# The 1e-9 of the softmax sums: an add on VectorE in place of an activation on ScalarE

## The chip, the cores and the metric

One core of one Trainium2 chip runs the kernel. The metric is the device time of one execution in microseconds (us), and the figure before is the median of 3 runs. The engines are TensorE (PE in the profile, with its weight loads as PEld), VectorE (DVE), ScalarE (ACT), GpSimd (POOL) and SyncE (SP, which here issues most DMAs).

## The reference

Attention with a local and a summary part, and then a gated feed-forward layer, all in float32:

```
B, H, S, D = 4, 8, 768, 64;  block, window = 32, 16
k_sum = max of k over blocks of 32 keys;  v_sum = mean of v over blocks of 32
scores_l = scale * q k^T, kept where |i - j| < 16, else -1e9
scores_s = scale * q k_sum^T + log(32)
a = exp(concat(scores_l, scores_s) - rowmax)
a = a / (sum(a) + 1e-9)
x = a @ concat(v, v_sum)            -> (4, 768, 512)
h = relu(x @ w_in)                  -> (4, 768, 1024)
conv = 3-tap convolution of h along the sequence, per channel
out = (h * sigmoid(conv)) @ w_out   -> (4, 768, 512)
```

The weights of the feed-forward layer come as 64-bit floats. The kernel decodes them to float32 on the chip.

## The kernel before, in words

The sequence of each of the 4 batches is cut into two halves, which gives 8 chunks of 384 positions (c = 0 to 7). A chunk has 4 pairs of heads, so there are 32 pairs (n = 4c + p, n = 0 to 31). Attention works on blocks of 64 queries; each block sees a window of 96 keys and the 24 summary keys, 120 columns.

For one pair, `qk` (L248) issues 24 small matmuls (L260) of queries against keys into two PSUM tiles `pq`, one per head, and calls `softmax` (L271). For each of the two heads and three column groups, VectorE adds the mask and finds the row's extreme (L278, the value goes to `nm`), and ScalarE takes the exponential with the row sum accumulated into one column of `sm` (L288; the profile shows an ACTIVATE and a read of the accumulator for each). That gives six sums per row, in the 128x6 tile `sm`. ScalarE then adds 1e-9 to all six (L296), VectorE takes the reciprocal (L297), and the exponentials are multiplied by it (L300), on VectorE for the pairs 0 to 3 and on GpSimd for all others. `tr` (L304) transposes them on TensorE (L308) and copies them out (L313, L315); `av` (L320) multiplies by the values (L329), and the result is split into a high and a low part, `xh` on ScalarE (L349) and `xl` on VectorE (L350).

The feed-forward layer uses split numbers: `f1` (L393) multiplies three products of high and low parts (L404) per block of 128 columns; `gate_conv` (L415) applies relu (L422) and the convolution (L425 or L427, then L434 twice); `gate_mul` (L444) does tanh (L451), the product (L452), and the split into `ghi` on ScalarE (L455) and `glo` on GpSimd (L456); `f2` (L462) does the last matmul (L473) and ScalarE writes it out (L482). The weights are decoded and split by `weights` (L124): ScalarE L97, VectorE L100, L101, L104, ScalarE L127, GpSimd L128. `vmean_pair` (L221) and `prep_pair` (L202) make the summary values and keys (VectorE L228 and L210, ScalarE L236, GpSimd L217, L213 and L238).

The order of the work. The program lists the work in units; each unit calls `slot(j)` (L359), in which even j start a pair's `qk` and odd j prepare the next pair, then `slot_t` (transposes of the group two slots before, DEPTH = 2) and `slot_av`, the feed-forward pieces of the unit, and a part of the gate work that is left over. Chunk 0's four pairs come first, before any feed-forward work (L507 to L516). Semaphores are put in by the framework, and the framework also orders the instructions of each engine, by data dependences, the place in the source and estimated durations. Only for chunks 2 to 7 (`ORDERED` is 2) is TensorE's order the order of the source:

```
        if c < ORDERED:
            for u in range(NFC):
                unit(c, u, pieces, False)
        else:
            with tc.manual_schedule(engines={mybir.EngineType.PE}):
                for u in range(NFC):
                    unit(c, u, pieces, True)
```

All other engines, and TensorE in chunks 0 and 1, get their order from the framework. Matmuls on a zero tile (L78, `warm`) stand between the early work. The tiles `sm` and `nm` have 3 buffers each, the exponentials `a` have 4. Each engine works through its queue in order, so an instruction that waits holds up what is behind it on that engine.

Of the kernel before, what the change touches and what calls it, by code (L numbers as in the profile page):

```python
# [10 lines left out]
AF = mybir.ActivationFunctionType  # L11
ALU = mybir.AluOpType
# [38 lines left out]
def attention_ffn(ctx, tc, qT, kT, vT, v4, w_in, cwT, w_out, mask8, ident_in, out):  # L51
    nc = tc.nc
# [195 lines left out]
    def qk(c, p):  # L248


        st = state[(c, p)]
        n = c * NP + p
        pq = [
            ps.tile([P, 512], F32, tag="s", name=f"pq{n}_{h}", bufs=2) for h in range(2)
        ]
        for blk in range(CB):
            i, half = divmod(blk, 2)
            for h in range(2):
                r = slice(h * QB, (h + 1) * QB)
                last = nc.tensor.matmul(  # L260
                    pq[h][half * QB : (half + 1) * QB, i * NK : (i + 1) * NK],
                    st["q"][r, blk * QB : (blk + 1) * QB],
                    st["kw"][r, blk, :],
                    start=True,
                    stop=True,
                )
        if c == 0:
            warm(f"pq{p}", ins(last))
        softmax(n, c % 2, pq)

    def softmax(n, hf, pq):  # L271
        nm = sp.tile([P, 2, 3], F32, tag="nm", name=f"nm{n}", bufs=3)
        sm = sp.tile([P, 2, 3], F32, tag="sm", name=f"sm{n}", bufs=3)
        for h in range(2):
            a = sp.tile([P, 3, NK], F32, tag="a", name=f"a{n}_{h}", bufs=DEPTH + 2)
            state[("a", 2 * n + h)] = a
            for i in range(3):
                nc.vector.tensor_tensor_reduce(  # L278
                    a[:, i, :],
                    pq[h][:, i * NK : (i + 1) * NK],  # L280
                    mask[:, hf, i, :],
                    -0.125,
                    3.0e38,
                    ALU.add,
                    ALU.min,
                    nm[:, h, i : i + 1],
                )
                nc.scalar.activation(  # L288
                    a[:, i, :],
                    a[:, i, :],  # L290
                    AF.Exp,
                    bias=nm[:, h, i : i + 1],
                    scale=-1.0,
                    accum_out=sm[:, h, i : i + 1],
                )
        nc.scalar.activation(sm, sm, AF.Copy, bias=1e-9)  # L296
        nc.vector.reciprocal(sm, sm)  # L297
        for h in range(2):
            a = state[("a", 2 * n + h)]
            (nc.gpsimd if n >= NP else nc.vector).tensor_tensor(  # L300
                a, a, sm[:, h, :].unsqueeze(2).to_broadcast([P, 3, NK]), ALU.mult
            )
# [377 lines left out]
```

## Time and profile before

| | |
|---|---|
| median of 3 runs | 408.15 us (404.59 to 409.48) |
| the profiled execution | 408.03 us, its span 406.2 us |
| granted TensorE clock, mean over the span | 0.986 of full |
| busy: TensorE, its weight loads | 386.4 us, 319.5 us |
| busy: VectorE, ScalarE, GpSimd | 261.3, 254.2, 151.6 us |
| L296: ScalarE, 32 times | 6.6 us busy |
| L297: VectorE, 32 times | 5.9 us busy |
| bytes moved by DMA | 54.47 MB, 134 GB/s on average |

The span runs from the first instruction to the last of one profiled execution; the execution's own time lies 1.8 us above it. All times inside the profile count from the span's start. A busy time sums an engine's instructions; neighbours on one engine can overlap by a tenth of a microsecond, so the start of the next instruction tells more of the engine's pace than the end of the last. The idle time of an engine counts only where the chain of waits runs over it.

### The profile page before, as it was taken

What the parts mean: (1) busy time and instruction counts of PE and PEld (TensorE: products, weight loads), DVE (VectorE), ACT (ScalarE), POOL (GpSimd) and SP (SyncE); (2) the same over time, 40 slices, a digit from 0 to 9 for tenths busy, and PEclk for the clock granted to TensorE, in tenths of its full rate; (3) what the DMA queues carried; (4) which work ended last, traced back from release to release, by engine and by line L of the source; (5) the groups of instructions that cost most, each with busy time, mean ns of one, the idle gap of its engine ahead of it and who ended that gap; (6) DMA issues with size and microseconds to landing.
All of it is one profiled execution on the core that took longest, in us unless ns stands there. A gap on an engine that the chain in (4) does not pass through costs nothing.

```text
span 406.2 us, 8829 instructions
## 1 busy us (share of the span) xinstructions
PE 386.4 (95%) x3164; PEld 319.5 (79%) x3173; DVE 261.3 (64%) x777; ACT 254.2 (63%) x806; POOL 151.6 (37%) x179
## 2 busy tenths in 40 slices
PE   7978869999799999999999999999999999999996
PEld 3546657886678888888888888888788888999884
DVE  4899789998965765668765456466565665556200
ACT  3664799998777677766565777756655654343211
POOL 2327464585953333322432333333332242222200
PEclk9999699999989999999999999999999999999999
DMA  8999863766966774646332344334220000000011
GB/s 290 327 361 211 230 177 115 248 202 192 252 162 205 235 217 123 190 145 192 78 92 78 80 111 112 104 96 117 67 63 28 27 2 26 26 27 26 28 52 52
DMA packets 60715, 54.47 MB, mean 134 GB/s; under 512 B 24640, under 2 KB 51328, under 8 KB 60672
## 3 DMA queue, kind: packets, MB, share of 16 engines
q1 hardware_dynamic: 56928, 47.19, 41.3%
q10 hardware_dynamic: 3744, 6.73, 4.5%
q8 instruction: 25, 0.41, 0.4%
q14 instruction: 18, 0.15, 0.1%
HBM read 45.55 MB, written 6.29 MB: 128 GB/s over the span
## 4 chain that ended last, share of the span: by engine, by line
PE 68%; ACT 11%; DVE 10%; DMA 3%; issue 3%; POOL 3%; SPq 0%; ACTq 0%; DVEq 0%; POOLq 0%
PE f L404 26%; PE f L473 26%; PE pq L260 5%; ACT a L288 5%; PE xp L329 4%; PE pt L308 4%; DVE t L434 3%; PE pw L78 2%; ACT t L451 1%; DMA kw<-kT 1%; DMA k_xh<-kT 1%; ACT f L422 1%; DVE t L452 1%; POOL wout_lo L128 1%; ACT t L425 1%
## 5 line engine op out<-in xcount | busy, mean ns | idle before, releaser
L456 POOL TENSOR_TENSOR glo<-t,ghi 128x383 fp32r<-128x383 f32 (+1 forms) x64 | 66.6, 1041 | 116.3 <-ACT ghi L455 111.8
L434 DVE SCALAR_TENSOR_TENSOR t<-f,cw,t 128x382 f32<-128x382 f32 (+3 forms) x128 | 78.8, 616 | 23.5 <-ACT t L425 20.7
L404 PE MATMUL f<-xh,win_hi 128*128 128x384 f32 (+1 forms) x256 | 93.0, 363 | 0.9 <-ACT win_hi L127 0.9
L404 PE MATMUL f<-xl,win_hi 128*128 128x384 f32 (+1 forms) x256 | 87.7, 343 | 0.0
L404 PE MATMUL f<-xh,win_lo 128*128 128x384 f32 (+1 forms) x256 | 86.9, 340 | 0.0
L473 PE MATMUL f<-wout_lo,ghi 128*128 128x512 f32 x192 | 76.1, 396 | 3.1 <-POOL wout_lo L128 3.1
L288 ACT ACTIVATE a<-a,nm 128x120 f32<-128x120 f32 x192 | 73.3, 384 | 9.1 <-DVE nm L278 8.8
L473 PE MATMUL f<-wout_hi,ghi 128*128 128x512 f32 x192 | 76.3, 398 | 0.2 <-ACT ob L482 0.2
L473 PE MATMUL f<-wout_hi,glo 128*128 128x512 f32 x192 | 75.1, 392 | 0.0
L451 ACT ACTIVATE t<-t 128x383 f32<-128x383 f32 (+1 forms) x64 | 33.6, 525 | 60.4 <-DVE t L434 59.3
L300 POOL TENSOR_TENSOR a<-a,sm 128x360 f32<-128x360 f32 x56 | 45.8, 839 | 64.4 <-DVE sm L297 36.5
L452 DVE SCALAR_TENSOR_TENSOR t<-t,f 128x383 f32<-128x383 f32 (+1 forms) x64 | 35.3, 552 | 28.2 <-ACT t L451 28.2
L404 PEld LDWEIGHTS f<-xh,win_hi 128*128 128x128 f32 x256 | 48.7, 190 | 3.6 <-issue 1.3
L404 PEld LDWEIGHTS f<-xl,win_hi 128*128 128x128 f32 x256 | 49.0, 191 | 0.9 <-issue 0.3
L404 PEld LDWEIGHTS f<-xh,win_lo 128*128 128x128 f32 x256 | 48.8, 191 | 0.2
L278 DVE CUSTOM_DVE_ANT_0 a<-pq,mask 128x120 f32<-128x120 f32 x192 | 42.7, 276 | 1.9 <-PE pq L260 1.9
L473 PEld LDWEIGHTS f<-wout_lo,ghi 128*128 128x128 f32 x192 | 36.3, 189 | 9.7 <-POOL wout_lo L128 4.1
L455 ACT CAST ghi<-t 128x383 fp32r<-128x383 f32 (+1 forms) x64 | 32.6, 509 | 16.6 <-DVE t L452 15.9
L473 PEld LDWEIGHTS f<-wout_hi,glo 128*128 128x128 f32 x192 | 36.2, 188 | 7.7
L473 PEld LDWEIGHTS f<-wout_hi,ghi 128*128 128x128 f32 x192 | 36.1, 188 | 7.3 <-issue 0.6
L308 PE MATMUL pt<-ident,a 128*120 128x128 f32 x192 | 34.0, 285 | 5.4 <-ACT aT L315 3.7
L260 PEld LDWEIGHTS pq<-kw,q 64*64 64x64 f32 x768 | 23.9, 134 | 18.6 <-issue 13.0
(59 smaller groups left out, 505.8 us busy)
## 6 DMA issues: line engine op xcount, KB each, us to landing
va<-v SPq DMA_DIRECT2D x32, 288.0 KB
kw<-kT SPq DMA_DIRECT2D x28, 288.0 KB
q<-qT SPq DMA_DIRECT2D x32, 192.0 KB
out_dram<-ob ACTq DMA_DIRECT2D x24, 256.0 KB
kT<-kT SPq DMA_DIRECT2D x12, 392.0 KB
vt<-vT SPq DMA_DIRECT2D x12, 384.0 KB
wo<-w_out SPq DMA_DIRECT2D x8, 512.0 KB
raw_a<-w_in SPq DMA_DIRECT2D x6, 512.0 KB
```

What stands on the lines that cost most here:

```text
L260: last = nc.tensor.matmul(pq[h][half * QB : (half + 1) * QB, i * NK : (i + 1) * NK], st["q"][r, blk * QB : (blk + 1) * QB], st["kw"][r, bl ...
L278: nc.vector.tensor_tensor_reduce(a[:, i, :], pq[h][:, i * NK : (i + 1) * NK], mask[:, hf, i, :], -0.125, 3.0e38, ALU.add, ALU.min, nm[:, h ...
L288: nc.scalar.activation(a[:, i, :], a[:, i, :], AF.Exp, bias=nm[:, h, i : i + 1], scale=-1.0, accum_out=sm[:, h, i : i + 1],)
L300: (nc.gpsimd if n >= NP else nc.vector).tensor_tensor(a, a, sm[:, h, :].unsqueeze(2).to_broadcast([P, 3, NK]), ALU.mult)
L308: last = nc.tensor.transpose(pt[:NK, i * P : (i + 1) * P], a[:, i, :], ident)
L404: last = nc.tensor.matmul(ph[:, :n], w[:, fc, cc, :], x[:, cc, :n], start=(cc == 0 and m == 0), stop=(cc == NCC - 1 and m == 2),)
L434: nc.vector.scalar_tensor_tensor(t[:, i0:i1], h[:, hf + k - 1 + i0 : hf + k - 1 + i1], cw[:, fc, k : k + 1], t[:, i0:i1], ALU.mult, ALU.add,)
L451: nc.scalar.activation(t, t, AF.Tanh, scale=0.5)
L452: nc.vector.scalar_tensor_tensor(t, t, 1.0, h[:, hf : hf + ng], ALU.add, ALU.mult)
L455: nc.scalar.copy(hi, t)
L456: nc.gpsimd.tensor_tensor(gated["lo"][:, fc, d0 : d0 + ng], t, hi.bitcast(F32), ALU.subtract)
L473: nc.tensor.matmul(po, gx[:, fc, ss], w[:, fc, :], start=(fc == 0 and m == 0), stop=(fc == NFC - 1 and m == 2),)
```

## The change

The addition of 1e-9 to the six sums of a pair is done by VectorE, as a tensor-scalar add in place on the same tile, where ScalarE did it as a copy with a bias. The reciprocal, on VectorE before and after, follows it directly in the source.

```
-        nc.scalar.activation(sm, sm, AF.Copy, bias=1e-9)
+        nc.vector.tensor_scalar(sm, sm, 1e-9, None, ALU.add)
         nc.vector.reciprocal(sm, sm)
         for h in range(2):
             a = state[("a", 2 * n + h)]
```

## Rows read from the trace of the kernel before

**Rows 1.** The page's first part, of the whole span: for each engine its busy time in us, the share of the span and the number of instructions.
```profile
PE 386.4 (95%) x3164; PEld 319.5 (79%) x3173; DVE 261.3 (64%) x777; ACT 254.2 (63%) x806; POOL 151.6 (37%) x179
```

**Rows 2.** The table of busy times by stretch, stretches between 20 and 300 us: the stretch, its length, the busy time of each engine in us (instructions), then TensorE's granted clock as a share of full speed, the mean busy share of the DMA engines, GB/s.
```profile
20.00:30.00 10.00, 8.00 (x94) 4.61 (x95) 9.71 (x30) 6.94 (x25) 1.96 (x2) 1.00 1.04 362
40.00:50.00 10.00, 8.06 (x43) 6.11 (x43) 8.66 (x34) 7.37 (x31) 4.80 (x6) 0.66 0.84 221
44.00:49.00 5.00, 5.00 (x21) 3.65 (x18) 4.16 (x13) 2.74 (x15) 2.27 (x2) 0.50 0.74 218
50.00:60.00 10.00, 6.91 (x108) 5.26 (x108) 7.23 (x31) 9.24 (x32) 6.69 (x8) 1.00 0.77 201
60.00:90.00 30.00, 29.79 (x296) 23.83 (x299) 28.29 (x86) 27.93 (x95) 17.44 (x22) 1.00 0.57 177
150.00:300.00 150.00, 148.18 (x1330) 128.87 (x1328) 92.05 (x298) 99.19 (x323) 53.15 (x69) 1.00 0.40 110
```

**Rows 3.** The list of who waited for whom, whole span: engine, tile and line that waited, what it waited for, us in total, times, the longest.
```profile
DVE sm L297 <- ACT sm L296: 4.8, 6, 2.6
...
PE pt L308 <- POOL a L300: 0.3, 1, 0.3
```

**Rows 4.** The groups of instructions by line, ScalarE's group of L296 and VectorE's of L297: line, engine, operation, out<-in, shapes, count, then busy us and mean ns of one, then idle time just before them and what ended it.
```profile
L296 ACT ACTIVATE sm<-sm 128x6 f32<-128x6 f32 x32 | 6.6, 206 | 0.0
...
L297 DVE RECIPROCAL sm<-sm 128x6 f32<-128x6 f32 x32 | 5.9, 184 | 5.0 <-ACT sm L296 4.8
```

**Rows 5.** The timeline around one pair of the late part, 148 to 157 us (ScalarE, POOL, TensorE): start in us, duration in us, engine, line, operation, out<-in, shapes, count, and in brackets the engine's idle time before it and what ended that.
```profile
148.07 0.19 ACT L288 ACTIVATION_READ_ACCUMULATOR a<-a,nm 128x1 f32 x1
...
148.52 0.21 ACT L296 ACTIVATE sm<-sm 128x6 f32<-128x6 f32 x1
148.63 0.46 ACT L315 COPY aT<-pt 120x384 f32<-120x384 f32 x1
...
149.46 1.54 POOL L300 TENSOR_TENSOR a<-a,sm 128x360 f32<-128x360 f32 x2 [4.15 <-ACT f L422]
...
156.54 0.32 PE L308 MATMUL pt<-ident,a 128*120 128x128 f32 x1
```

**Rows 6.** The timeline around pair 2, ScalarE and VectorE, 19.4 to 20.3 us, columns as in the group before.
```profile
19.39 0.19 ACT L288 ACTIVATION_READ_ACCUMULATOR a<-a,nm 128x1 f32 x1
...
19.84 0.21 ACT L296 ACTIVATE sm<-sm 128x6 f32<-128x6 f32 x1
...
20.08 0.19 DVE L297 RECIPROCAL sm<-sm 128x6 f32<-128x6 f32 x1 [0.95 <-ACT sm L296]
```

**Rows 7.** The chain of waits that ended last, two of its pieces: start in us, its part of the chain in us, engine, tile and line.
```profile
26.28 0.18 DVE sm L297
...
56.29 0.21 ACT sm L296
```

**Rows 8.** VectorE's timeline, small instructions between 15 and 46 us, columns as above.
```profile
15.42 0.56 DVE L313 COPY aT<-pt 120x384 f32<-120x384 f32 x1 [0.76 <-PE pt L308]
...
18.97 0.16 DVE L100 TENSOR_SCALAR wl_cw<-cw_words 128x24 uint32<-128x24 uint32 x1
...
24.84 0.17 DVE L101 SCALAR_TENSOR_TENSOR cw<-cw,wl_cw 128x24 uint32<-128x24 uint32 x1
25.05 0.18 DVE L104 SCALAR_TENSOR_TENSOR cw<-cw_words,cw 128x24 uint32<-128x24 uint32 x1
...
45.20 0.19 DVE L297 RECIPROCAL sm<-sm 128x6 f32<-128x6 f32 x1
45.30 0.24 DVE L278 CUSTOM_DVE_ANT_0 a<-pq,mask 128x120 f32<-128x120 f32 x1
```

**Rows 9.** The timeline of VectorE (first two rows) and of POOL (last three), 11 to 126 us: VectorE's and POOL's instructions that overlap, columns as above.
```profile
35.46 1.28 DVE L344 CAST xl<-xl 128x8 fp32r<-128x8 f32 x1
...
125.01 0.19 DVE L297 RECIPROCAL sm<-sm 128x6 f32<-128x6 f32 x1 [2.63 <-ACT sm L296]
...
11.11 0.82 POOL L238 COPY va<-vm 24x768 f32<-24x768 f32 x1
...
35.41 1.31 POOL L128 TENSOR_TENSOR win_lo<-wu_i,win_hi 128x512 fp32r<-128x512 f32 x1 [1.29 <-ACT win_hi L127]
...
124.94 1.03 POOL L456 TENSOR_TENSOR glo<-t,ghi 128x385 fp32r<-128x385 f32 x1 [2.98 <-ACT ghi L455]
```

**Rows 10.** TensorE's timeline, three instructions that began after an idle stretch, columns as above.
```profile
42.15 0.32 PE L260 MATMUL pq<-kw,q 64*64 64x120 f32 x2 [1.94 <-issue]
...
58.31 0.29 PE L308 MATMUL pt<-ident,a 128*120 128x128 f32 x1 [2.73 <-ACT aT L315]
...
110.41 0.50 PE L473 MATMUL f<-wout_lo,ghi 128*128 128x512 f32 x1 [2.44 <-POOL wout_lo L128]
```

**Rows 11.** The timeline around pair 11, 102 to 105 us (ScalarE, VectorE, POOL), columns as above.
```profile
102.06 0.19 ACT L288 ACTIVATION_READ_ACCUMULATOR a<-a,nm 128x1 f32 x1
...
104.49 0.18 DVE L297 RECIPROCAL sm<-sm 128x6 f32<-128x6 f32 x1
...
104.74 0.79 POOL L300 TENSOR_TENSOR a<-a,sm 128x360 f32<-128x360 f32 x1 [0.73 <-DVE sm L297]
```

**Rows 12.** ScalarE's timeline around 10.5 us, columns as above.
```profile
10.40 0.27 ACT L236 ACTIVATE vm<-pv 24x128 f32<-24x128 f32 x1
10.57 0.19 ACT L296 ACTIVATE sm<-sm 128x6 f32<-128x6 f32 x1
```

More of the change, by code (lines that the diff above doesn't have):

```diff
@@ L295, in softmax @@
                 )
-        nc.scalar.activation(sm, sm, AF.Copy, bias=1e-9)
+        nc.vector.tensor_scalar(sm, sm, 1e-9, None, ALU.add)
         nc.vector.reciprocal(sm, sm)
```

## The prediction

> **What bounds the kernel now.** I read the page first: TensorE (PE) is busy for 95% of the span, VectorE (DVE) and ScalarE (ACT) for 64% and 63% [rows 1]. The reader is to see there that neither engine of the change is the bound as an average. An average hides stages, so the table by stretch comes next [rows 2]. From 150 to 300 us PE has 1.8 us of idle time in 150. In 20 to 30 us it has 2.0 and in 50 to 60 us 3.1, while DVE (9.71 of 10) and then ACT (9.24) are nearly full. From 60 to 90 us all three are nearly full. One more stall, of 2.44 us, ends at 110.41 us [rows 10]. The granted clock is 0.66 of full in 40 to 50 us; within that it is 0.50 from 44 to 49 us, the 1.2 GHz level [rows 2], after PE had stood still for 1.94 us before 42.15 us [rows 10]. The list of waits comes third: PE waited only 0.3 us for the normalised softmax (L300 on POOL) in the whole span [rows 3]. So the change can move the end almost only in the first 125 us, and there only where a softmax pair stands on the chain of waits, which I read last.
>
> **The change part by part.** There are 32 pairs (n = 0 to 31), with one L296 and one L297 each [rows 4].
>
> What it removes. L296 takes 206 ns on ACT [rows 4], but the next instruction starts 0.11 us after it (148.52 and 148.63 us [rows 5]), so ACT gets back about 32 x 0.11 = 3.5 us. One hand-over between engines stays, now from the last sum to the add.
>
> What it adds. The trace has no DVE add of 128x6. The nearest rows are a tensor-scalar of 128x24 with 0.16 us, the reciprocal with 0.18, and, for two small DVE instructions of which the second needs the first, the step from 24.84 to 25.05 us: 0.21 us [rows 8]. I take 0.21 us from add to reciprocal, as these operands are nearest in size. The lower bound is the step from a reciprocal to the next, independent instruction, 0.10 us (45.20 to 45.30 us [rows 8]). The upper bound is 1.28 us, a cast of 8 columns beside a POOL instruction [rows 9]; that is rival 1. On DVE this sums to 32 x 0.21 = 6.7 us, of which few places count.
>
> What it moves. The add needs the last exponential's sum, not L296, and L296 did not follow that sum at once: at 148 us the sum is there at 148.26, L296 starts at 148.52 behind another ACT instruction, and POOL multiplies from 149.46 [rows 5]. So the add can start up to 0.3 us sooner than L296 did. DVE's wait does not grow: before, L297 waited for L296 4.8 us in all, in 6 cases of 32 [rows 3]. Queued behind it on DVE are the convolution (L427, L434) and the next exponents' inputs (L278); ACT and POOL wait for those.
>
> Now the places, against the profiled execution's own 408.03 us (its span of 406.2 and 1.8 around it; the median of the runs is 408.15, so there is no shift to make).
> - Pairs 14 to 31: POOL ends the two multiplications at 151.00 us and PE first transposes one of them two units later, at 156.54 us [rows 5]. These 5.5 us cover both 0.21 us more on DVE and an earlier start. ACT's 0.11 us can matter where PE waits for ACT at all, in the 1.8 us of idle time named above. I take -0.2, bounds -1.8 and 0.
> - Pairs 0 and 1: DVE idles 0.76 us before its copy at 15.42 us [rows 8], which takes both steps of 0.21. Nothing; without that cover +0.4.
> - Pair 2, on the chain: the last sum ends at 19.58, L296 starts at 19.84 and L297 at 20.08, and DVE had been idle for 0.95 us [rows 6]. With the add at 19.62 the reciprocal starts at 19.83: -0.25, bounds -0.4 and 0.
> - Pair 3, on the chain with L297 at 26.28 us [rows 7], where DVE is full [rows 2]: +0.2, bounds 0 and +0.2.
> - Pair 4: L297 at 45.20 us stands between the inputs of the next exponents [rows 8], and POOL follows: +0.1, bounds -0.5 (if the add goes ahead of these) and +0.2.
> - Pair 6: L296 is on the chain at 56.29 us [rows 7], in ACT's run that PE waits 2.73 us for until 58.31 us [rows 10]. One ACT step less: -0.1, bounds -0.36 and 0.
> - Pair 5, where PE runs on at half clock, and 7 to 10, where it is full [rows 2]: nothing.
> - Pair 11: the last sum is there at 102.25, L297 runs only at 104.49 behind a weight decode, POOL idles 0.73 us and multiplies from 104.74; behind that, in POOL's order, come the weights for which PE idles 2.44 us until 110.41 [rows 10, 11]. An add that asks straight after the sum may pass the decode, and POOL's 0.73 us go. If it stays where L297 is, +0.2. I take -0.5.
> - Pairs 12 and 13: PE runs on. Nothing.
> Sum: -0.2 - 0.25 + 0.2 + 0.1 - 0.1 - 0.5 = -0.75 us; the bounds add up to -3.8 and +1.0. Forecast: 408.03 - 0.75 = 407.3 us. What is late next is what is late now: ACT's run to 58 us and the weight splits at 110 us.
>
> **A rule that speaks against it.** First the rows: a cast of 8 columns took 1.28 us from 35.46 us on, beside a POOL instruction of 1.31 us that had begun at 35.41; a reciprocal at 125.01 us, inside a POOL instruction that had begun at 124.94, took 0.19 as ever [rows 9]. The Trainium skill ("SBUF — State Buffer", section "Who interferes with whom") says that VectorE's copy, cast and tensor-scalar, from SBUF to SBUF, can take a pair of ports that GpSimd uses too, and that whichever comes second waits out the other's whole instruction; the reciprocal is not in its list. The trace agrees in both cases. By this the add would pay where the reciprocal behind it does not, which gives rival 1; without it the sum is as above.
>
> **Rivals.**
> 1. Slower: the add waits for a running POOL instruction, as that cast did, and DVE stands behind it. In 10 of the 32 pairs (0, 1, 3, 5, 8 to 13) POOL is running at some time between the last sum and L297 (the first and the last of them in [rows 9]); in the late pairs POOL idles until the multiplication itself (4.15 us before 149.46 [rows 5]), so nothing is paid there. All ten at 1.28 us on the chain would give 408.03 + 12.8 = 420.8; with PE busy in six of them, four count: 408.03 + 4 x 1.28 = 413.2. It decides once 0.75 us of such waits fall on the chain. For it: rows 9. Against it: most of the ten lie where PE has work.
> 2. Slower by another order. The instructions do not run in the order of the source: vmean's copy (L236, at 10.40 us) ran ahead of L296 (10.57), and it is later in the source [rows 12]. The order is worked out from estimated durations, and PE's is fixed by the program only from chunk 2 on. A ready time that moves by 0.1 us may reorder the first 125 us. Price: one stall like that of 2.73 us [rows 10] and one more stretch like that of 10 us at a clock of 0.66, 3.4 us lost [rows 2]: +6.1, about 414 us.
> 3. The same to the good: the stall of 2.44 us [rows 10] and the half-clock stretch go: -5.8, about 402.2 us. For both: two such stalls stand in the present order, so another can have one more or one less. Against both: the last two thirds, where PE's order is fixed, cannot take part.
>
> **How the numbers follow.** Forecast 0.60 (its own range, by the spread of the runs from 404.6 to 409.5, is 405 to 410), rival 1 0.12, rival 2 0.13, rival 3 0.15. The likeliest gives 407.3. A range of 402.5 to 412.5 leaves out some 0.07 below and 0.12 above. A measurement here can tell about 2%, 8.2 us. Under 400.0 needs more than rival 3: 0.04. Over 416.3 needs rival 1 near its upper end or rival 2 with a second stall: 0.06. The rest, 0.90, is within 2%.
>
> **What would show it.** Right: 32 adds of about 0.16 us on DVE, ACT's busy time down by 6.6 us and DVE's up by about 5; L300 of the late pairs 0.3 to 0.6 us sooner after the last sum and no change in PE's pace there; PE's idle time in the first 125 us within 2 us of now. Wrong: adds of 1 us and more (rival 1); another number of half-clock stretches or of stalls over 2 us before 125 us (rivals 2 and 3); a change of length after 150 us by more than the 1.8 us of idle time there, which would break the reading that PE alone sets the pace.

## The result, and the profile after

The changed kernel takes 409.69 us (median of 20 runs, 408.12 to 413.55), the kernel before 408.01 us (20 runs beside it, 404.51 to 410.07). The ratio over all runs is 1.0072 with a 95% interval of 1.0042 to 1.0101, which is about 2.9 us slower, where 0.75 us faster was forecast; the medians lie only 1.7 us apart, the means of the runs 3.0 us. All profiles below are of single executions; the changed kernel's took 410.21 us, its span is 408.4 us. The mean granted clock of this execution and of the one before is the same, 0.986.

A first look at where the time goes. The table gives the end of a unit (its twelfth L404 matmul on TensorE), read off each trace: for the kernel before in us, for the others as the distance from it.

| end of | before | changed | e11 | e12 | e6 | e7 |
|---|---|---|---|---|---|---|
| unit 3 | 61.73 | +1.15 | +1.23 | +0.77 | +3.22 | +0.10 |
| unit 8 | 83.41 | +0.76 | +0.92 | +0.96 | +3.23 | +0.11 |
| unit 10 | 91.81 | +0.21 | +0.93 | +0.38 | +3.23 | +0.11 |
| unit 11 | 96.86 | +3.20 | +0.93 | +3.22 | +3.23 | +0.11 |
| unit 15 | 126.20 | +3.12 | +1.11 | +2.88 | +2.65 | +0.06 |
| unit 39 | 258.41 | +2.61 | +0.90 | +2.71 | +2.64 | -0.41 |
| last instruction | 406.15 | +2.27 | +0.21 | +2.36 | +2.24 | -1.11 |

The second column is the changed kernel; the other four are experiments told below. The loss is there by 126 us, most of it falls on unit 11, between 92 and 100 us, and 0.85 us come back behind it. TensorE's idle time confirms it: from its first instruction to 130 us it sums to 12.9 us in the trace of before and to 16.4 us in that after; behind 130 us it is 2.0 and 1.3 us.

The page's first part of the changed kernel, to be put beside [rows 1]:

```profile
PE 385.8 (94%) x3173; PEld 319.2 (78%) x3173; DVE 269.9 (66%) x809; ACT 251.8 (62%) x774; POOL 150.7 (37%) x179
```

VectorE has 8.6 us more, ScalarE 2.4 us less; TensorE's work is the same. The table by stretch, as [rows 2], of three of its stretches:

```profile
40.00:50.00 10.00, 6.68 (x72) 4.88 (x71) 8.64 (x35) 8.59 (x33) 4.74 (x6) 1.00 0.95 253
...
60.00:90.00 30.00, 29.88 (x274) 24.18 (x273) 27.12 (x84) 25.64 (x86) 16.09 (x20) 0.96 0.54 163
...
150.00:300.00 150.00, 148.70 (x1295) 129.94 (x1294) 94.71 (x308) 100.82 (x321) 52.70 (x69) 1.00 0.43 116
```

From 150 to 300 us TensorE is as full as before. In 40 to 50 us this execution ran at full clock where the one before ran at half for much of the time, and in 60 to 90 us a little slower: where the half-speed stretches fall differs, so the profiles can't be compared stretch by stretch without the clock beside them.

The groups of L296 and L297, as [rows 4], and the waits, as [rows 3]:

```profile
L296 DVE TENSOR_SCALAR sm<-sm 128x6 f32<-128x6 f32 x32 | 6.9, 216 | 30.5 <-ACT a L288 30.5
L297 DVE RECIPROCAL sm<-sm 128x6 f32<-128x6 f32 x32 | 6.0, 188 | 0.7
```

```profile
POOL a L300 <- DVE sm L297: 51.4, 22, 4.8
DVE sm L296 <- ACT a L288: 30.5, 23, 2.1
...
PE pt L308 <- POOL a L300: 3.1, 2, 1.7
PE pq L260 <- POOL kw L217: 3.1, 2, 1.7
```

The mean add is 216 ns; the median one takes 171 ns, as two of the 32 take 0.56 and 1.24 us. VectorE now waits 30.5 us in 23 places for a last exponential, where it waited 4.8 us in 6 for L296. TensorE's wait for L300 rose from 0.3 to 3.1 us. A late pair, as [rows 5]:

```profile
151.41 0.19 ACT L288 ACTIVATION_READ_ACCUMULATOR a<-a,nm 128x1 f32 x1
151.63 0.17 DVE L296 TENSOR_SCALAR sm<-sm 128x6 f32<-128x6 f32 x1 [1.19 <-ACT a L288]
151.84 0.19 DVE L297 RECIPROCAL sm<-sm 128x6 f32<-128x6 f32 x1
152.20 1.53 POOL L300 TENSOR_TENSOR a<-a,sm 128x360 f32<-128x360 f32 x2 [3.55 <-DVE sm L297]
```

The add comes 0.03 us behind the last sum, the reciprocal 0.21 us later, and POOL multiplies 0.60 us after that sum where it was 1.20 us [rows 5]. Late pairs do what the prediction said. Early pairs do not. VectorE and POOL around pair 5 and, for pair 11, VectorE and POOL as [rows 11]:

```profile
49.14 1.41 POOL L128 TENSOR_TENSOR win_lo<-wu_i,win_hi 128x512 fp32r<-128x512 f32 x1 [0.60 <-ACT win_hi L127]
49.34 1.24 DVE L296 TENSOR_SCALAR sm<-sm 128x6 f32<-128x6 f32 x1
50.50 0.68 DVE L101 SCALAR_TENSOR_TENSOR wu_i<-wu_i,wl_i 128x512 uint32<-128x512 uint32 x1
51.10 0.18 DVE L297 RECIPROCAL sm<-sm 128x6 f32<-128x6 f32 x1
...
104.77 0.16 DVE L296 TENSOR_SCALAR sm<-sm 128x6 f32<-128x6 f32 x1
...
105.55 1.04 DVE L101 SCALAR_TENSOR_TENSOR wu_o<-wu_o,wl_o 128x512 uint32<-128x512 uint32 x1
...
106.51 0.18 DVE L297 RECIPROCAL sm<-sm 128x6 f32<-128x6 f32 x1
```

Two things are to be seen. At pair 5 the add began while POOL was at work and ended 0.03 us after POOL's instruction (50.58 against 50.55 us). And the framework puts other work between add and reciprocal: here a decode, and at pair 11 a convolution and a decode, so that the reciprocal ends 1.9 us after its add began. The order of the lists moved more than that: the last sums of the pairs 4, 5 and 8 to 11 themselves are there 1.4 to 2.3 us later than before, ahead of their own adds. TensorE behind its idle stretches, as [rows 10]:

```profile
52.61 0.54 PE L308 MATMUL pt<-ident,a 128*120 128x128 f32 x3 [1.69 <-POOL a L300]
57.71 0.52 PE L308 MATMUL pt<-ident,a 128*120 128x128 f32 x3 [2.08 <-ACT aT L315]
93.72 0.85 PE L260 MATMUL pq<-kw,q 64*64 64x120 f32 x24 [1.70 <-POOL kw L217]
...
112.44 0.50 PE L473 MATMUL f<-wout_lo,ghi 128*128 128x512 f32 x1 [1.87 <-POOL wout_lo L128]
```

The wait for kw at 92 us is new. What held kw up is in POOL's timeline, first of the changed kernel, then of the kernel before:

```profile
91.47 1.48 POOL L456 TENSOR_TENSOR glo<-t,ghi 128x383 fp32r<-128x383 f32 x1 [2.49 <-ACT ghi L455]
92.89 0.77 POOL L217 COPY kw<-ks 128x144 f32<-128x144 f32 x1
```

```profile
83.94 0.82 POOL L217 COPY kw<-ks 128x144 f32<-128x144 f32 x1
84.72 1.55 POOL L456 TENSOR_TENSOR glo<-t,ghi 128x383 fp32r<-128x383 f32 x1
```

The same cast stood ahead of two gate splits (L456) and now stands behind them, and ahead of the last of them POOL itself waited 2.49 us for ScalarE. Nor could the cast have run ahead of 91.49 us in any case, as what it reads, VectorE's maximum over the blocks of keys (L210), had moved as well; the kernel before, then the changed one:

```profile
81.54 0.94 DVE L210 TENSOR_REDUCE ks<-kT 128x24 f32<-128x768 f32 x1
...
90.55 0.94 DVE L210 TENSOR_REDUCE ks<-kT 128x24 f32<-128x768 f32 x1
```

Nobody wrote that down: the framework put all lists into another order. Up to about 38 us they are the same but for the add; from there to about 130 us they differ on all five engines, behind that in single places of VectorE's and ScalarE's.

### The profile page after: what moved, and what is told of

It reads as the page before. It is cut to its first block, busy times and chain, and to the rows that moved or that the text cites. A ratio compares the mean times of both kernels' runs of the same rounds, so it can differ in the third digit from the quotient of the medians.

```text
span 408.4 us, 8852 instructions
## 1 busy us (share of the span) xinstructions
PE 385.8 (94%) x3173; PEld 319.2 (78%) x3173; DVE 269.9 (66%) x809; ACT 251.8 (62%) x774; POOL 150.7 (37%) x179
## 4 chain that ended last, share of the span: by engine, by line
PE 62%; ACT 14%; DVE 13%; POOL 5%; issue 4%; DMA 1%; SPq 0%; ACTq 0%; POOLq 0%; DVEq 0%
PE f L473 26%; PE f L404 23%; ACT a L288 6%; PE pt L308 4%; PE xp L329 4%; PE pq L260 4%; DVE t L434 4%; ACT t L451 2%; PE pw L78 2%; POOL glo L456 2%; DVE t L452 1%; POOL a L300 1%; DMA k_xh<-kT 1%; ACT ghi L455 1%; POOL wout_lo L128 1%
## 5 line engine op out<-in xcount | busy, mean ns | idle before, releaser
L456 POOL TENSOR_TENSOR glo<-t,ghi 128x383 fp32r<-128x383 f32 (+1 forms) x64 | 66.8, 1044 | 128.5 <-ACT ghi L455 124.4
L404 PE MATMUL f<-xh,win_hi 128*128 128x384 f32 (+1 forms) x256 | 93.4, 365 | 0.9 <-ACT win_hi L127 0.9
L404 PE MATMUL f<-xl,win_hi 128*128 128x384 f32 (+1 forms) x256 | 87.8, 343 | 0.0
L404 PE MATMUL f<-xh,win_lo 128*128 128x384 f32 (+1 forms) x256 | 87.3, 341 | 0.0
L300 POOL TENSOR_TENSOR a<-a,sm 128x360 f32<-128x360 f32 x56 | 45.4, 832 | 55.2 <-DVE sm L297 51.4
L404 PEld LDWEIGHTS f<-xh,win_hi 128*128 128x128 f32 x256 | 49.1, 192 | 3.6 <-ACT win_hi L127 1.2
L404 PEld LDWEIGHTS f<-xl,win_hi 128*128 128x128 f32 x256 | 49.2, 192 | 0.7 <-issue 0.2
L404 PEld LDWEIGHTS f<-xh,win_lo 128*128 128x128 f32 x256 | 48.9, 191 | 0.2
L455 ACT CAST ghi<-t 128x383 fp32r<-128x383 f32 (+1 forms) x64 | 32.5, 508 | 16.4 <-DVE t L452 15.6
```

Of the source, the lines that this page charges most:

```text
L300: (nc.gpsimd if n >= NP else nc.vector).tensor_tensor(a, a, sm[:, h, :].unsqueeze(2).to_broadcast([P, 3, NK]), ALU.mult)
L404: last = nc.tensor.matmul(ph[:, :n], w[:, fc, cc, :], x[:, cc, :n], start=(cc == 0 and m == 0), stop=(cc == NCC - 1 and m == 2),)
L455: nc.scalar.copy(hi, t)
L456: nc.gpsimd.tensor_tensor(gated["lo"][:, fc, d0 : d0 + ng], t, hi.bitcast(F32), ALU.subtract)
```

## The experiments

Theories. **P**: early adds on VectorE wait for a running GpSimd instruction, and that is the price (rival 1 of the prediction). **Q**: each add costs by its own length, since VectorE's queue has no slack in the first 125 us. **O**: the price is the new order of the lists (rival 2). **G**: it is the instructions between add and reciprocal. The expectations also speak of D (the add on VectorE costs, by P or Q), E (it costs in the early pairs) and W (the wait for kw is the price of the new order); "the first run of this study" is e1, "the last" the experiment just before. To hold an order, dependences without a semaphore were put between neighbours of each engine's list; "old order" is that of the kernel before, with VectorE's add directly ahead of its reciprocal, "new order" that of the changed kernel (code shortened):

```
+        tc.add_manual_dep(here[k], here[previous].name, DependencyInfo(NoSync, DATA), reason="order")
```

Each ratio is to the kernel before on the same chip; e1 to e4, e5 to e8, e9 to e12 and e13 to e18 ran on four different chips. The clock is the mean granted clock over the runs of the kernel; for the kernel before it is 0.987 to 0.990. Neither kernel was run unchanged with its order held; e7 and e16, the same line held and free, differ by 0.0015, within their intervals, so the holding itself shows no price.

| run | adds on VectorE | lists | ratio, 95% interval | clock |
|---|---|---|---|---|
| e16 | 14 to 31 | free | 0.9960, 0.9925 to 0.9994 | 0.989 |
| e7 | 14 to 31 | old | 0.9975, 0.9937 to 1.0013 | 0.989 |
| e4 | none, no add at all | old | 0.9982, 0.9954 to 1.0009 | 0.987 |
| e10 | ten that do not wait | old | 1.0008, 0.9974 to 1.0042 | 0.987 |
| e11 | all | new to 74 us, then old | 1.0036, 1.0007 to 1.0065 | 0.987 |
| e8 | all, tensor_tensor | old | 1.0048, 1.0015 to 1.0081 | 0.983 |
| e1 | all | old | 1.0049, 1.0015 to 1.0082 | 0.984 |
| e6 | 0 to 13 | old | 1.0058, 1.0023 to 1.0093 | 0.982 |
| changed | all | free (new) | 1.0072, 1.0042 to 1.0101 | 0.985 |
| e5 | all | new, kw back | 1.0088, 1.0050 to 1.0127 | 0.985 |
| e13 | all but 5 | new | 1.0091, 1.0052 to 1.0130 | 0.979 |
| e3 | all, next to reciprocal | new | 1.0101, 1.0068 to 1.0133 | 0.985 |
| e12 | all | old to 74 us, then new | 1.0123, 1.0068 to 1.0178 | 0.978 |
| e9 | all, twice | old | 1.0124, 1.0073 to 1.0174 | 0.982 |
| e2 | none, ScalarE adds | new | 1.0170, 1.0109 to 1.0230 | 0.980 |
| e15 | all | new to 74 us, then old but ScalarE's | 1.0188, 1.0141 to 1.0235 | 0.978 |
| e18 | ten | new from 74 to 90 us only | 1.0230, 1.0204 to 1.0257 | 0.979 |
| e14 | all | new; VectorE's, GpSimd's, SP's old from 74 us | 1.0256, 1.0194 to 1.0317 | 0.976 |
| e17 | all | new from 74 to 90 us only | 1.0307, 1.0266 to 1.0349 | 0.968 |

### Edit and order crossed: e1 to e4

e1, the edit in the old order:

```
-        nc.scalar.activation(sm, sm, AF.Copy, bias=1e-9)
+        nc.vector.tensor_scalar(sm, sm, 1e-9, None, ALU.add)
         (old order)
```

> The change's edit (VectorE adds the 1e-9 directly ahead of its reciprocal, in all 32 pairs), but every engine's list of instructions otherwise held in the order of the kernel before. Theory O (the loss comes from the new order of the five lists, not from the add): ratio to before 0.998 to 1.003, and the end of unit 14 within 1 us of before. Theory D (the add on VectorE costs what was lost, by its waits for GpSimd and its queue): 1.005 to 1.009, with unit 14 about 3 us late as in the changed kernel.

e2, the reverse: before's line, new order.

> The other half of the same crossing: ScalarE adds the 1e-9 as before, directly behind the last exponential of its pair, and every list is otherwise held in the order of the changed kernel. Theory O: ratio to before 1.004 to 1.010, unit 14 about 3 us late. Theory D: 0.997 to 1.003, unit 14 within 1 us of before.

e3, the changed kernel, with the reciprocal next to its add:

```
 VectorE's list:  add, [decode or convolution], reciprocal  ->  add, reciprocal, [decode or convolution]
```

> The changed kernel in its own order, except that in the 24 pairs where another VectorE instruction stands between the add and the reciprocal, the reciprocal is put directly behind the add. Theory G (the instruction in between, 0.5 to 1.7 us in pairs 1, 3, 5, 7 to 11, is what delays the normalised weights and with them the end): 0.7 to 2 us come back against the changed kernel, ratio to before 1.002 to 1.005. Theory O with its cause elsewhere in the lists: as the changed kernel, 1.005 to 1.010.

e4, no add at all:

```
-        nc.scalar.activation(sm, sm, AF.Copy, bias=1e-9)
```

> Leaves out the addition of 1e-9 altogether (neither engine does it); all other instructions in the order of the kernel before. It prices the add itself on either engine in that order. All theories: ratio to before 0.997 to 1.000; the add off the critical path in most pairs gives at most 0.2 us for each of the few early pairs whose chain it ends (about -0.5 us in all). Under theory D it would be at least 2 us below the first run of this set, under theory O within 1 us of it.

e1 gave 1.0049, above what theory O alone allows, and e4 lies 1.0049 - 0.9982 = 0.0067 (2.7 us) below it, the intervals apart: the add on VectorE has a price even where the order does not change. e2 gave 1.0170, more than either theory expected, so the new order is worse still with ScalarE's add in it: a list made for one placement does not serve the other. e3 gave nothing back (1.0101 against 1.0072), and G falls.

What e1's price is made of shows in its trace, VectorE and POOL at two places:

```profile
26.20 0.95 POOL L238 COPY va<-vm 24x768 f32<-24x768 f32 x1 [4.57 <-ACT vm L236]
26.38 0.80 DVE L296 TENSOR_SCALAR sm<-sm 128x6 f32<-128x6 f32 x1
...
116.49 1.12 POOL L456 TENSOR_TENSOR glo<-t,ghi 128x385 fp32r<-128x385 f32 x1 [3.80 <-ACT ghi L455]
116.65 0.98 DVE L296 TENSOR_SCALAR sm<-sm 128x6 f32<-128x6 f32 x1
```

Each add that starts within a POOL instruction ends with it (27.18 against 27.15 us, 117.63 against 117.61). Four of the first 14 do so here, at pairs 0, 3, 10 and 12, with 0.36, 0.80, 0.99 and 0.98 us; the other 28 take 0.16 to 0.17.

### Which pairs, and which form: e5 to e8

e5, one chain of the new order put back:

```
 VectorE's list:  L210 of the kw pair ahead of the weight decode (17 places earlier)
 GpSimd's list:   L217, its cast, ahead of L456, L128, L217, L456 (4 places earlier)
```

> The changed kernel with two instructions of one chain back at their old places: the PSUM copy (line 210, VectorE) of one head pair's keys, and the GpSimd cast (line 217) that makes kw of it, for which TensorE waits from 92.0 to 93.7 us in the changed kernel. Theory W (the new order loses its share by this wait): the wait of 1.70 us is gone, unit 11 ends 1.2 to 1.7 us sooner than in the changed kernel, ratio to before 1.002 to 1.005. Rival (another operand is as late, the cast weights or a pair's normalised exponentials): the wait comes back under another name within 10 us, and the ratio stays at 1.005 to 1.010.

e6 and e7, the add split by pairs, in the old order (e7 with n >= 14):

```
-        nc.scalar.activation(sm, sm, AF.Copy, bias=1e-9)
+        if n < 14: nc.vector.tensor_scalar(sm, sm, 1e-9, None, ALU.add)
+        else: nc.scalar.activation(sm, sm, AF.Copy, bias=1e-9)
```

> Old order; VectorE adds in pairs 0 to 13 only, ScalarE in 14 to 31. Theory E (the add costs where VectorE's queue has no slack, in the first 125 us): as with all 32 on VectorE, 1.002 to 1.008. Rival (the cost is spread over all pairs, or is made after 125 us): 0.999 to 1.003.

> Old order; ScalarE adds in pairs 0 to 13, VectorE in 14 to 31. Theory E: 0.997 to 1.001. Rival: 1.002 to 1.006. Either way the first 125 us are those of the kernel before.

e8, another form:

```
-        nc.vector.tensor_scalar(sm, sm, 1e-9, None, ALU.add)
+        nc.vector.tensor_tensor(sm, sm, eps, ALU.add)     (eps: a 128x6 tile of 1e-9, set once at the start)
```

> VectorE's add in another form in the old order: tensor_tensor with a tile of 1e-9 in place of tensor_scalar with a constant (one more memset at the start). Theory P (what costs are the adds that wait for a GpSimd instruction under way: 3 of the first 14 took 0.8 to 1.0 us in the first run of this study): if this form does not wait, all adds take 0.15 to 0.25 us and the ratio falls to 0.998 to 1.003. Theory Q (each add costs by its own 0.16 to 0.2 us in a queue without slack): 1.002 to 1.008, as with tensor_scalar, however short the longest add is.

e6 and e7 part cleanly: 1.0058 with early adds, 0.9975 with late ones, and their intervals do not meet. The whole price lies in the first 14 pairs. The rows at pair 3 show how it is paid; first e6, then e7 (in both, lines behind 296 stand one lower, so L298 is the reciprocal, L301 the multiplication, L330 the product with the values; e7's ScalarE add ran at 25.83 us):

```profile
26.10 0.94 POOL L238 COPY va<-vm 24x768 f32<-24x768 f32 x1 [4.57 <-ACT vm L236]
26.28 0.80 DVE L296 TENSOR_SCALAR sm<-sm 128x6 f32<-128x6 f32 x1
...
27.11 0.19 DVE L298 RECIPROCAL sm<-sm 128x6 f32<-128x6 f32 x1
27.22 0.53 DVE L351 TENSOR_TENSOR xl<-xp,xh 128x384 fp32r<-128x384 f32 x1
...
27.85 0.30 PE L330 MATMUL xp<-aT,va 120*64 120x64 f32 x2 [0.95 <-POOL va L238]
```

```profile
26.25 0.91 POOL L238 COPY va<-vm 24x768 f32<-24x768 f32 x1 [4.61 <-ACT vm L236]
26.39 0.18 DVE L298 RECIPROCAL sm<-sm 128x6 f32<-128x6 f32 x1
26.58 0.56 DVE L351 TENSOR_TENSOR xl<-xp,xh 128x384 fp32r<-128x384 f32 x1
...
27.24 0.30 PE L330 MATMUL xp<-aT,va 120*64 120x64 f32 x2 [0.28 <-POOL va L238]
```

The add waits out L238, so the reciprocal is 0.72 us later, the split xl behind it in VectorE's queue 0.64 us later, and TensorE 0.61 us later: 0.95 us of idle time in place of 0.28. The bracket names va, but that copy had ended at 27.04 us, 0.8 us before TensorE went on in e6; xl, which reads the xp before it out of PSUM, ended at 27.75 and 27.14, 0.10 us before the matmul in both, and is what it most likely waited for. The victim is not the softmax but what is queued behind it. In the next microseconds the granted clock differs too, by the table by stretch, first e6, then e7:

```profile
30.00:33.00 3.00, 2.67 (x27) 2.07 (x28) 1.98 (x4) 1.78 (x4) 1.98 (x2) 0.50 1.10 331
```

```profile
30.00:33.00 3.00, 2.84 (x35) 1.86 (x32) 2.89 (x6) 1.22 (x3) 2.74 (x2) 1.00 1.14 315
```

In e6 TensorE stood idle twice (0.95 us before 27.85 us, then 1.00 us before 29.15 us) and ran at half speed, 1.2 GHz, from 30 to 33 us; in e7, with the second of these alone, it kept full speed. But the two idle stretches did not decide it. e1's execution has them as well, and its clock stayed full:

```profile
27.96 0.30 PE L329 MATMUL xp<-aT,va 120*64 120x64 f32 x2 [0.95 <-POOL va L238]
...
29.26 0.54 PE L308 MATMUL pt<-ident,a 128*120 128x128 f32 x3 [1.00 <-DVE aT L313]
```

```profile
30.00:33.00 3.00, 3.00 (x35) 1.95 (x34) 2.89 (x6) 1.99 (x4) 1.96 (x2) 1.00 1.09 335
```

Of the six traces with 0.9 us and more at both places (e1, e6, e8, e9, e12, e17) the clock fell near 30 us in e6, e8 and e17; of the fourteen others it did so in e15 alone. Over all runs the mean clock falls from 0.989 (e7) to 0.982 (e6).

e8's adds by tensor_tensor wait as long as those by tensor_scalar, and the ratio is the same, 1.0048. Its rows at the same place:

```profile
25.83 0.94 POOL L238 COPY va<-vm 24x768 f32<-24x768 f32 x1 [4.57 <-ACT vm L236]
26.00 0.78 DVE L296 TENSOR_TENSOR sm<-sm,eps 128x6 f32<-128x6 f32 x1
```

So the form is no way out, and as the waits stayed, this run does not tell P from Q. The Trainium skill ("SBUF — State Buffer", section "Who interferes with whom") says that a VectorE instruction with two inputs in SBUF contends with a GpSimd instruction that reads SBUF; this trace agrees, with 0.78 us.

e5: the wait for kw went, and nothing was gained (1.0088). (L210 takes a maximum over blocks of keys in SBUF; the expectation calls it a copy from PSUM, which it is not.) Unit 11 ended at 99.91 us, 0.14 us sooner than in the changed kernel. Its rows show what took the place:

```profile
83.96 0.28 PE L234 MATMUL pv<-ident,vs 128*24 128x128 f32 x1 [0.98 <-DVE xl L350]
...
94.32 0.54 PE L308 MATMUL pt<-ident,a 128*120 128x128 f32 x3 [1.11 <-POOL a L300]
```

### Price of a wait, place of the order: e9 to e12

e9 and e10, in the old order:

```
+        nc.vector.tensor_scalar(sm, sm, 5e-10, None, ALU.add)       (twice; e9)
+        if n in (1, 2, 4, 5, 6, 7, 8, 9, 11, 13): (VectorE adds)    (else ScalarE; e10)
```

> Old order; VectorE adds twice (half of the 1e-9 each time) in all 32 pairs, one directly behind the other: 14 more instructions of 0.16 us in the first 125 us, 2.3 us of VectorE's time, or more where the second waits for GpSimd too. Theory Q (VectorE's time in that stretch is what the end pays, 0.5 to 0.8 us for each): 1.2 to 1.9 us above one add in the same order, ratio to before 1.007 to 1.011. Theory P (the few adds that wait for GpSimd are the price, and the second add waits no more): as one add, 1.003 to 1.006.

> Old order; VectorE adds in ten of the first 14 pairs; in the four whose add waited for GpSimd in the old order (0, 3, 10 and 12: 0.36, 0.80, 0.99, 0.98 us) and in 14 to 31 ScalarE does. That leaves 1.7 of the 4.8 us of VectorE's early adds. Theory P: 0.998 to 1.001. Theory Q: a third of the cost, 1.001 to 1.003. Neither holds if it stays at 1.005.

e11 and e12 cross the two orders at 74 us; the add is on VectorE throughout:

```
 e11: every list = new order up to unit 6, old order behind it
 e12: every list = old order up to unit 6, new order behind it
```

> The changed kernel (VectorE adds in all pairs), its lists in the new order up to the place about 74 us in where both orders have issued the same instructions on every engine, and in the old order from there. If the new order loses its part between 92 and 100 us (there the changed kernel falls 3 us behind the first run of this study): TensorE does not wait for kw at 92 us, unit 11 ends within 1 us of that run, ratio to before 1.002 to 1.006. If the loss is made ahead of 74 us: 1.006 to 1.010.

> The same crossing the other way: old order up to about 74 us, new order from there, VectorE adds in all pairs. If the new order loses its part behind 74 us: the wait for kw at 92 us is there, unit 11 ends about 3 us late, ratio to before 1.007 to 1.011. If ahead of it: 1.002 to 1.006.

e10 points to P but does not show it: without the four adds that wait the ratio is 1.0008, though ten early adds are left, none above 0.18 us. By Q alone a third of e1's 0.0049 would be left, 0.0017, and the interval holds that too, and it overlaps e1's. e9 gave 1.0124, beyond both. Its trace says why: doubled adds meet POOL more often (seven waits of 0.35 to 1.23 us), and the adds of the first 14 pairs sum to 9.8 us in place of 4.8. A dose of adds is a dose of waits, so it does not refute P, and it does not part P from Q either.

e11 and e12 do part: 1.0036 and 1.0123, intervals just disjoint (1.0065 and 1.0068; e12 has six runs). The second share of the loss, that of the new order, is made behind 74 us. e12 repeats the changed kernel's wait to 0.02 us, and e11 has none there:

```profile
93.91 0.84 PE L260 MATMUL pq<-kw,q 64*64 64x120 f32 x24 [1.72 <-POOL kw L217]
```

### What stayed open: e13 to e18

e13, the changed kernel's one long wait taken away (n == 5 on ScalarE, in the new order):

```
+        if n != 5: (VectorE adds)  else: (ScalarE adds)
```

> The changed kernel in its own order, but pair 5's add, the one that waited 1.24 us at 49.34 us, is back on ScalarE behind that pair's last exponential. Theory P: its wait delays GpSimd's multiplication (51.4 us) and TensorE (idle 50.9 to 52.6 us); that idle time shrinks by 0.6 us or more, unit 3 ends about 1 us sooner, and 0.5 to 1.2 us come back: ratio to before 1.003 to 1.006. Rival (the order behind 74 us takes all of it anyway): unit 3 sooner, but unit 14 within 0.5 us of the changed kernel, ratio 1.006 to 1.010.

e14 and e15, between the changed kernel and e11, list by list:

```
 e14: from 74 us the lists of VectorE, GpSimd and SP old
 e15: from 74 us TensorE's old as well, ScalarE's alone new
```

> The changed kernel, with the lists of VectorE, GpSimd and SP in the old order from about 74 us on; TensorE's and ScalarE's stay new throughout. If the second share sits in VectorE's and GpSimd's lists: as e11, 1.002 to 1.006, no wait of TensorE over 1.5 us between 90 and 95 us. If in TensorE's or ScalarE's: 1.006 to 1.012.

> As the last, with TensorE's list old from about 74 us on too: ScalarE's alone is new there. If the share sits in TensorE's list: 1.002 to 1.006 here and more in the last. If in ScalarE's: 1.006 to 1.012 here too, unit 11 about 2 us late or more.

e16, e7's line with the order left to the framework:

> ScalarE adds in pairs 0 to 13, VectorE in 14 to 31, with no order prescribed: TensorE's, GpSimd's and SP's lists come out as before, and VectorE's and ScalarE's differ only behind 140 us. The first 125 us as before, ratio 0.995 to 1.001. It is the candidate that takes the part of the change that costs nothing.

e17 and e18, the new order from 74 to 90 us alone; e18 with e10's choice of pairs:

```
 every list = old to 74 us, new to 90 us, old behind it
```

> VectorE adds in all pairs; old order, but with the lists of the new order from about 74 to about 90 us (the softmax of pairs 9 and 10 and what lies beside it); both ends are places where the two orders have issued the same instructions on every engine. If the second share is made there: TensorE waits for kw at about 92 us by 1.5 to 1.9 us, unit 11 ends 3 us late, ratio to before 1.007 to 1.013. If it is made behind 90 us: 1.003 to 1.006, as the first run of this study.

> The last kernel with ScalarE's add in pairs 0, 3, 10, 12 and 14 to 31, whose adds waited for GpSimd in the old order or cost nothing either way. If the two shares add up: 0.003 to 0.006 below the last, at 1.003 to 1.008. If the order costs only together with the waits: 0.998 to 1.003.

e13: 1.0091, no gain, and unit 3 was no sooner (+1.44 us). VectorE and POOL at the place of the wait (here too L298 is the reciprocal):

```profile
49.64 1.27 POOL L128 TENSOR_TENSOR win_lo<-wu_i,win_hi 128x512 fp32r<-128x512 f32 x1 [0.84 <-ACT win_hi L127]
49.78 1.68 DVE L101 SCALAR_TENSOR_TENSOR wu_i<-wu_i,wl_i 128x512 uint32<-128x512 uint32 x1
51.38 0.18 DVE L298 RECIPROCAL sm<-sm 128x6 f32<-128x6 f32 x1
```

The wait is handed on: the decode behind the add now meets POOL, takes 1.68 us in place of 0.68, and the reciprocal is no sooner. In the changed kernel's own order taking that one add away gives nothing back.

e14 (1.0256) and e15 (1.0188) are worse than either end and than anything expected of them: such mixtures make losses of their own, so they do not say whose list the second share belongs to. e17 (1.0307) is again worse than either parent: there TensorE waits 5.3 us for kw at 92 us. It expected 1.013 at most, so it does not place the share between 74 and 90 us; joined to the old order, that piece makes its own, larger wait. But e18 is the stronger evidence for P: it has e17's lists and ten early adds, none of which waits in its trace, where four do in e17's (pairs 0, 3, 5 and 12; 0.65 to 1.24 us), and it is 0.0077 faster, 2.8 us by the medians (420.65 and 417.84 us), the intervals apart. By Q the four early adds that it moves back would give 0.7 us at 0.17 us each, and the late pairs, also back on ScalarE, nothing in its favour (e7). Its ratio itself, 1.0230, lies above both that were expected, so the two shares do not simply add up there.

e16: 0.9960, faster by 1.6 us (0.2 to 3.1), with TensorE's, GpSimd's and SP's lists the same as before. It is the best of the versions, but by little: its interval just leaves out 1, and that of e7, the same line in the held order, holds it.

## Why the prediction was wrong

The size of the steps was right where the add stands alone; the places were wrong.

- **Costs of the add.** 0.16 to 0.17 us, and 0.21 us from add to reciprocal [rows 8]: as said. VectorE's 8.6 us are 6.9 of adds and 1.7 of other instructions made longer, mostly decodes and casts (L101, L104, L344). ScalarE's 2.4 us miss the 6.6 named as a sign; the text's own 0.11 us for each, 3.5 us, was nearer, as neighbours overlap.
- **"DVE's wait does not grow"**: wrong, 30.5 us in place of 4.8. Of that 24.9 us lie behind 126 us, where the changed kernel gains time, so by itself the wait costs nothing there; before 126 us it is 5.6 us in 4 places, and e1, which waits only 2.7 us in all, loses its 0.0049 without it.
- **Pairs 14 to 31, -0.2**: the changed kernel gains 0.85 us behind unit 15, e7 1.2 us. Right in sign and within its bounds, four times too small or more.
- **Pairs 0 and 1, nothing**: pair 0's add waited 0.56 us for a POOL instruction and the reciprocals came 0.45 and 0.52 us later, but pair 2's last sum only 0.10 us later. Right.
- **Pair 2, -0.25**: the reciprocal came 0.17 us sooner (19.91 against 20.08 [rows 6]). **Pair 6, -0.1**: 0.21 sooner (56.32 against 56.53). Right in sign.
- **Pair 3, at most +0.2**: 0.22 us sooner in the changed kernel (26.06 against [rows 7]), but 0.64 us for the work behind it wherever the add fell into L238 (e6). The bound left out the price of [rows 9], which the same text gave to rival 1.
- **Pair 4, +0.1**: from the last sum to the reciprocal it took 0.94 us less than before, but the sum itself came 1.97 us later (45.91 against 43.94 us), as a weight decode (L97) that waited 1.25 us for POOL now stands ahead of the pair's exponentials in ScalarE's list. TensorE then waited 1.42 us for POOL's multiplication, before 47.40 us.
- **Pair 11, -0.5: failed.** The add did ask straight after the sum (104.53, 104.77 us), but it was the reciprocal that had to pass the decode, and that came behind it: 106.51 us, 1.98 us after the sum in place of 2.24 [rows 11]. POOL's idle time ahead of the multiplication stayed at 0.73 us:

```profile
106.77 1.99 POOL L300 TENSOR_TENSOR a<-a,sm 128x360 f32<-128x360 f32 x2 [0.73 <-DVE sm L297]
```

- **Pairs 5 and 7 to 10, nothing: failed.** "PE runs on" was read from the old order. In the new one the reciprocals come later by 1.86 (pair 5), 0.33, 1.95, 1.31 and 2.64 us (7 to 10). For pairs 5 and 9 nearly all of that is there at the last sum; between sum and reciprocal pairs 7, 8 and 10 take 0.6, 0.5 and 1.0 us more than before. TensorE meets 1.69 us at 52.6 and 1.70 us at 93.7 us.

So the step that failed is the sum over places, -0.75 us: it took the lists' order and the places of their stalls as they were before the edit, and set the wait of an add for a GpSimd instruction at nothing. In its place stand rival 1 and rival 2, each given about one chance in eight. Of its own signs, TensorE's idle time grew by 3.5 us ahead of 130 us, more than the 2 us that it allowed (ahead of 125 us).

Rival 1's mechanism, adds that wait for GpSimd, stands in the traces, and the experiments speak for it as the price of the early adds: in the old order these cost 0.0049 to 0.0058 (2.0 to 2.4 us), and in another order 2.8 us go with the adds that wait (e18 against e17). Its size was 5.2 us. That four adds waited in e1, as many as it counted, is luck: it took four of ten overlaps as standing on the chain, while in e1 four adds met POOL at all, pairs 0, 3, 10 and 12, with 0.36 to 0.99 us each in place of 1.28. The wait at pair 10 was followed by nothing. That at pair 12 was paid, though the prediction had TensorE run on there: from the end of unit 14 to that of unit 15 e1, e6 and e8 fall back by 0.75 to 0.79 us against before, and e4 and e10, which lack this wait, by 0.19 and 0.20; all five ran at full clock there. e11 has the wait too, with TensorE at half speed from 113 to 117 us, and falls back by nothing.

Rival 2's mechanism is shown by e11 and e12: new lists behind 74 us, a new wait at 92 us, 1.0123 against 1.0036. Its size, +6.1 us, was about twice what came.

In the changed kernel the two do not simply add up. Its own order meets POOL with two adds only, and taking the longer of them away gains nothing (e13); the five kernels with the new order behind 74 us and their adds on VectorE (changed, e3, e5, e12, e13) lie at 1.0072 to 1.0123, the four with the old order there (e1, e6, e8, e11) at 1.0036 to 1.0058. Single intervals of the two groups overlap, their ratios do not: the order behind 74 us has a share of the changed kernel's loss, by e11's 1.0036 about half of it.

The clock has a part. Runs of both kernels at a mean clock of 0.985 to 0.988 take 408.3 us (20 runs beside e1 to e4, kernel before) and 409.8 us (4 runs, changed): 1.5 us apart, so about half of the 2.9 us shows at equal clock, and the rest as more time at half speed (0.985 on average, 0.989 before). With four runs that split is rough. For the early adds the same comparison leaves less: e1, e6 and e8 take 408.6, 408.7 and 408.8 us (2, 3 and 4 runs) where the kernel before takes 408.3 beside e1 (20 runs) and 408.2 beside e6 and e8 (24 runs), 0.2 to 0.7 us of the 2.0 to 2.4. So most of what the waiting adds cost comes as more time at half speed and not as delay alone. That the waits bring the half-speed stretches on is likely, as only the kernels differ, but no run shows how.

Open: which places of the new lists behind 74 us make their share. Putting back the one visible chain (e5) only moved the wait, and pieces of one order do not fit the other (e14, e15, e17). Why the framework's estimates lead to this order was not tried. Nor was it found why one execution of a kernel has more half-speed stretches than another.

## What to carry to other kernels

Ahead of moving a small instruction to an engine whose instructions wait for another's, as VectorE's adds did for GpSimd's here, look up what runs on that other engine at each place, and charge the wait to whatever is queued behind it, not to the moved instruction. Where a framework orders the lists, an edit at any place is an edit of all lists from there on: hold the order to measure the edit, and make the edit only where lists and end are not tight. Here that meant the late pairs alone (0.9960 and 0.9975), while the same line in the early pairs cost 0.6%. And look at the clock of many runs before a loss of under 1% is put down to the waits seen in one trace.

## What the runs showed of the hardware

- A VectorE add of six columns that began within a GpSimd instruction took until that one ended: 1.24, 0.80, 0.99, 0.98 us in place of 0.16 to 0.17, by tensor_scalar as by tensor_tensor (0.78 us). A scalar_tensor_tensor waits in the same way (1.68 us in place of 0.68, e13); the reciprocal did not (0.19 us, [rows 9]).
- The clock fell to 0.50 of full from 30 to 33 us in e6, where TensorE had stood idle for 0.95 and 1.00 us just before, and stayed full in e7, where it had stood for 0.28 and 1.00 us. It also stayed full in e1, with 0.95 and 1.00 us: the same idle stretches were followed by half speed in some executions (e6, e8, e17) and not in others (e1, e9, e12).
- Executions of one and the same kernel differ in their mean granted clock, and in time with it: the kernel before took 404.5 us at 0.996 and 409.5 us at 0.986 (e1's set).
